# Four units' attention values in one run of matmuls per tile, and loads held back by sums: a fused window attention and MoE kernel

## The chip, the cores and the metric

One core of a Trainium2 chip runs the whole program. The metric is the device time of one execution in microseconds (us), as the median of several runs. The profile is one execution of the same program. Engines: PE (matmuls), DVE (vector), ACT (activations), POOL (GpSimd), SP (issues DMAs).

## The reference

```python
q, k, v: (8, 8, 576, 64) float32        # batch, heads, sequence, head size
scores = q @ k.T / 8
scores = where(|i - j| <= 32, scores, -1e9)
x = softmax(scores) @ v                 # window attention
x = x.transpose(0, 2, 1, 3).reshape(4608, 512)
h = x @ w_in                            # (512, 2048)
g = h / (1 + exp(-1.702 * h))
out = g @ w_out                         # (2048, 512)
```

## The kernel before

**Units and tiles.** The 4608 rows are cut into 36 units of 128 rows and 9 tiles of four units. Per unit: keys and queries are loaded by POOL's DMA queue (`load_kq`, L141), transposed by SP's (`T_dma`, L235; `turn(u)` does queries u and keys u + 1), `scores` makes the 24 score matmuls, ACT takes the exponential, `band` masks it on DVE, and `values` multiplies by v. v lies in `self.ve`, loaded by `load_v` (L211); a second copy shifted by 64 rows lies in `self.vo` and is made on POOL by `odd_v` (L222, two copies a unit). Each of the 8 heads of a unit is two matmuls on half the columns of PE, 65 columns long (64 values and the sum of the weights). `norm` divides on DVE (L339, L340), and `x_T` transposes x by a DMA on SP (L352) or on PE (L356).

**The MLP.** For a tile, layer 1 (`l1_group`) runs four groups, n = 0 to 3. A group has seven products of four matmuls, in the order 1, 7, 6, 2, 5, 4, 3, in the PSUM banks A, C, B and E: ACT copies product 1 from A to B and product 7 out of C, DVE writes E = B + s7 (L484, after product 6) and C = B + s7 (L490, after product 5), and ACT makes the Gelu of A, E, C, B (L471). Product 5 writes B again, so it waits until L484 has read it; product 3 waits for L490 in the same way. Sums of x (`x_sums`, L400 and L401, once a tile) and of g (`g_sums`, L412 to L415, four after each group) feed these products and those of layer 2. Layer 2 is a list `self.l2` of single matmuls, worked off in portions: `do(l2, n)` issues the next n. It uses banks LA and LB.

**Order.** Everything is written out by hand; each engine does its instructions in this order. `front(t)` makes the scores of the next four units among 32 layer 2 matmuls; `back(t)` runs the four groups of tile t and, between them, the values of the next tile's units. With u = 4t + 4, `back` handles units u to u + 3. `SHARES` gives the layer 2 matmuls dealt out after products 1, 7, 2 and 5/4 (`fill(1)`, `fill(7)`, `fill(2)`, `fill(4)`); `side(0)` and `side(1)` put one DVE step (a mask or a sum) behind L484 and L490. `AHEAD` deals some before and after the values. Banks are shared: `values(u, "AC")` fills banks A and C, which the groups use for products, and `"t"` a double bank which the scores use as well. In tiles 3 to 7 the values of two units are one run ahead of group 1, and those of the other two one run ahead of group 3; in tile 2 each of the four is a run by itself.

**Loads.** `fetch(u)` issues loads of queries u, keys u + 1 and a v on POOL, as early as its place in the order and free buffers allow (five for queries and keys each, nine for v). POOL and SP work off their queues in order, so a copy or a DMA that waits holds all that stand behind it.

Of the kernel before, what the change touches and what calls it, by code (L numbers as in the profile page):

```python
# [15 lines left out]
F32 = mybir.dt.float32  # L16
BF16 = mybir.dt.bfloat16
F16 = mybir.dt.float16
# [8 lines left out]
class _Kernel:  # L27
# [55 lines left out]
    def setup(self):  # L83
        nc, cst = self.nc, self.cst
        self.ident = cst.tile([128, 128], BF16, name="ident")
        self.identh = cst.tile([128, 128], F16, name="identh")
        self.mask = cst.tile([128, 4, SQ], BF16, name="mask")
        self.bias = cst.tile([128, 512], BF16, name="bias")
        self.w1 = cst.tile([128, 4, self.DFF], F16, name="w1")
        self.w2 = cst.tile([128, 16, self.DM], F16, name="w2")  # L90
        self.a = {i: cst.tile([128, 2, 1024], F16, name=f"a{i}") for i in (1, 2, 3, 4)}
        self.b = {i: cst.tile([128, 8, 256], F16, name=f"b{i}") for i in (1, 2, 3, 4)}
        self.k_first = cst.tile([128, 4, 64], BF16, name="k_first")
        self.v_first = cst.tile([64, self.H, 66], BF16, name="v_first")
        self.ve = [cst.tile([128, self.H, 66], BF16, name=f"ve{i}") for i in range(9)]
        self.vo = [cst.tile([128, self.H, 66], BF16, name=f"vo{i}") for i in range(5)]
        self.spark = cst.tile([128, 1], F32, name="spark")

    def setup_mask(self):

# [105 lines left out]
    def load_v(self, u, which=slice(None)):  # L206
# [3 lines left out]
        for off, b, s, n in list(self.pieces(128 * u, 128))[which]:  # L210
            self.nc.gpsimd.dma_start(t[off:off + n, :, :self.D], self.v[b, :, s:s + n, :].rearrange("h s d -> s h d"))  # L211

    def odd_v(self, u, eng, parts=(0, 1)):

        vo = self.vo[u % (3 if u > 15 else 5)]
        nxt = self.v_first if u == self.NU - 1 else self.ve[(u + 1) % 9][0:64]

        def words(ap):
            return ap.rearrange("p h d -> p (h d)").bitcast(I32)

        for i in parts:
            eng.tensor_copy(*((words(vo[64:128]), words(self.ve[u % 9][64:128])), (words(vo[0:64]), words(nxt)))[i])  # L222
# [88 lines left out]
    def values(self, u, tag):  # L311

        D = self.D
        p = self.p.pop(u)
        if tag == "t":
            acc = self.bank(tag, name="pv")
            self.acc[u] = [acc]
            acc = [acc[:, 0], acc[:, 1]]
        else:
            acc = [self.bank(x, name="pv") for x in tag]  # L320
            self.acc[u] = [x.rearrange("p (b n) -> p b n", b=1) for x in acc]
        for h in range(self.H):
            o = slice((h % 4) * (D + 1), (h % 4 + 1) * (D + 1))
            for blk in range(2):
                vt = (self.ve[u % 9], self.vo[u % (3 if u > 15 else 5)])[blk]
                w = p[:, h % 2, h // 2 * 2 + blk, :] if len(p.shape) == 4 else p[:, h % 2, h // 4, h // 2 % 2, blk, :]
                self.mm(acc[h // 4][64 * blk:64 * blk + 64, o], w, vt[:, h, :D + 1],
                        start=(h % 4 == 0))

    def norm(self, u):  # L330
        dve, D = self.nc.vector, self.D
        x = self.x[u] = self.sb("x", [128, self.H, D], F16, 4)
        rec = self.sb("rec", [128, 2, 4, 1], F32, 3)
        at = 0
        for acc in self.acc.pop(u):
            n = acc.shape[1]
            acc = acc[:, :, 0:4 * (D + 1)].rearrange("p b (h e) -> p b h e", e=D + 1)
            r = rec[:, at:at + n]
            dve.reciprocal(r, acc[:, :, :, D:])  # L339
            dve.tensor_mul(x[:, 4 * at:4 * (at + n), :].rearrange("p (b h) d -> p b h d", b=n), acc[:, :, :, :D],  # L340
                           r.to_broadcast([128, n, 4, D]))
            at += n

    def x_T(self, u, tag=None, eng=None):
        nc = self.nc
# [198 lines left out]
    def layer2(self, pairs, last):  # L544
# [54 lines left out]
        for P in (6, 2, 4, 5, 3):  # L599
# [3 lines left out]

    SHARES = {("first", 1): (3, 0, 5, 4), ("first", 2): (0, 6, 6, 6), ("first", 3): (3, 1, 7, 7), ("last", 0): (0, 12, 6, 6),
              0: (4, 4, 6, 6), 1: (3, 3, 6, 6), 2: (0, 6, 5, 6), 3: (2, 2, 5, 5)}


    AHEAD = {1: (0, 6), 3: (2, 3)}  # L610

    def opening(self):

# [119 lines left out]
        self.x_T2(6, "t", dve)  # L733
        self.do(self.l2, 6)

    def fetch(self, u):
        self.load_kq("q", u)
        self.load_kq("k", u + 1)
        if u < 16:
            self.load_v(u + 1)  # L740
        elif u >= 18:
            self.load_v(u - 1)

    def spread(self, u):
        if 16 <= u < self.NU:
# [6 lines left out]
    @staticmethod  # L752
    def do(fs, n=99):
        for _ in range(min(n, len(fs))):
            fs.pop(0)()

    def front(self, t, late):

        l2, do = self.l2, self.do
        if t + 1 == self.NT:  # L760
            self.l2eng = self.nc.scalar
            do(late, 3)
            do(l2, 8)
            self.x_T(self.NU - 2, "t", self.l2eng)
            xs = self.x_sums(t)
            do(xs, 1)
            do(l2, 12)
            do(late)
            do(xs)
            return  # L770
        self.l2eng = self.nc.vector
        u = 4 * t + 4
        self.scores(u, "t")
        self.scores(u + 1, "AC")
        do(late, 2)
        do(l2, 20)
        do(late)
        xs = self.x_sums(t)
        do(xs, 1)
        self.scores(u + 2, "BE")  # L780
        self.scores(u + 3, "t")
        do(l2, 12)
        do(xs)

    def back(self, t):

        more = t + 1 < self.NT
        do, l2 = self.do, self.l2
        u = 4 * t + 4
        bands = [lambda i=i: self.band(u + i) for i in range(4)] if more else []  # L790
        dv = bands[0:2]
        for n in range(4):
            if (t, n) == (3, 1):
                self.turn(20)
            if (t, n) != (3, 0):
                self.turn(u + n + 4)
            if (t, n) not in ((2, 3), (3, 0), (3, 3)):
                self.fetch(u + n + 5)
            if t == 2 and n in (1, 3):
                self.values(u + n - 1, "t")  # L800
                self.norm(u + n - 1)
                self.x_T(u + n - 1)
            elif more and n in (1, 3):
                do(l2, self.AHEAD[n][0])
                self.values(u + n - 1, "AC")
                self.norm(u + n - 1)
                if u + n < self.NU - 1:
                    self.x_T(u + n - 1)
                self.values(u + n, "t")
                self.norm(u + n)  # L810
                self.x_T(u + n)
                do(l2, self.AHEAD[n][1])
            if (t, n) == (3, 0):
                self.fetch(20)
            self.spread(u + n + 2)
            if (t, n) == (3, 0):
                self.fetch(21)
            if (t, n) == (3, 3):
                self.fetch(24)

            key = ("first", n) if t == 2 else ("last", n) if not more else n
            share = dict(zip((1, 7, 2, 4), self.SHARES.get(key, (3, 3, 5, 5))))

            def fill(i):
                do(l2, share[i])
                self.l2eng = self.nc.scalar
                if t == 2 and n in (1, 3) and i == 7:
                    self.values(u + n, "t")
                    if n == 3:
                        self.norm(u + n)  # L830
                        self.x_T(u + n)
                if i == 4:
                    do(dv, 2 if (t, n) == (2, 2) else 99)

            def side(i):
                if (t, n, i) == (2, 1, 0):
                    self.norm(u + n)
                    self.x_T(u + n)
                else:
                    do(dv, 1)  # L840

            self.l1_group(t, n, fill, side)
            dv += bands[2:4] if n == int(t == 2) else []
            dv += self.g_sums(t, 2 * n, 2)
        return dv

    def run(self):
# [5 lines left out]
        more = self.layer2([(i, j) for i in range(1, self.NT) for j in range(2)][:-1], (self.NT - 1, 1))  # L853
        do = self.do
# [42 lines left out]
        self.seed2 = dve  # L897
        self.odd_v(14, pool)
        self.odd_v(15, pool)
        self.fetch(16)  # L900
        late = self.back(2)
        for t in range(3, self.NT):
            self.front(t, late)
# [74 lines left out]
```

## Time and profile before

| | |
|---|---|
| runs | 281.67 us median of 3 (281.62 to 282.94) |
| profiled execution | 281.27 us, span of the profile 279.5 us |
| granted PE clock | 0.999 |
| busy | PE 96%, DVE 75%, ACT 70%, POOL 48% |
| a steady tile (t = 3 to 7) | 27.64 us |

In the rows of the order of time: start in us, duration, engine, line, operation, output and inputs by the program's names, shapes, and the count of merged instructions; in brackets the idle time before and what ended it. Matmuls are pipelined, so each lasts longer than the distance to the next; what a stretch costs PE is read from starts. In the kernel's names h is a bank of layer 1, o one of layer 2, pv one of values, tp one of transposes.

### The profile page before, as it was taken

Reading aid. Unit: us, or ns where it says so; the run is one execution under the profiler, and the core shown is the slowest. Engines: PE = TensorE matmul, PEld = TensorE weight load, DVE = VectorE, ACT = ScalarE, POOL = GpSimd, SP = SyncE. Lnnn points to the kernel's source line nnn. Section 1 sums busy time; section 2 is a strip of 40 time slices with the busy share of each in tenths; the row PEclk is TensorE's granted clock in tenths of the full one; section 3 lists DMA queues with packets and bytes.
Section 4 is the critical chain, followed back from the end, with each engine's and each line's share of the span. In section 5 each row is a group of like instructions: output and inputs, shape, how many; then the busy total and the mean of one; then the engine's idle time right before and its main releaser. Section 6 shows DMA issues by size and latency. Waiting matters only on the chain.

```text
span 279.5 us, 8854 instructions
## 1 busy us (share of the span) xinstructions
PE 268.2 (96%) x3632; PEld 222.6 (80%) x3632; DVE 210.9 (75%) x491; ACT 195.4 (70%) x343; POOL 133.0 (48%) x199
## 2 busy tenths in 40 slices
PE   1989999999999999999999999999999999999995
PEld 1568656776888888888888888888888888888884
DVE  3454598897997798788888887888778887945731
ACT  2586893989897588758875877687759775568411
POOL 8894695999593554635684519442520100000000
PEclk9999999999999999999999999999999999999999
DMA  8999999999999999999999999999972050202023
GB/s 88 166 204 199 178 207 165 185 136 159 131 167 140 203 120 140 172 189 115 182 194 178 126 163 159 134 183 132 168 91 85 2 115 19 77 2 75 2 104 124
DMA packets 150265, 37.61 MB, mean 135 GB/s; under 512 B 138064, under 2 KB 145872, under 8 KB 150224
## 3 DMA queue, kind: packets, MB, share of 16 engines
q0 software_dynamic: 106656, 18.42, 95.5%
q1 hardware_dynamic: 43120, 18.10, 37.9%
q8 instruction: 28, 0.46, 0.7%
q10 hardware_dynamic: 448, 0.52, 0.6%
q14 instruction: 13, 0.11, 0.1%
HBM read 36.83 MB, written 9.44 MB: 166 GB/s over the span
## 4 chain that ended last, share of the span: by engine, by line
PE 90%; DMA 4%; POOL 3%; ACT 1%; issue 1%; POOLq 0%
PE o L70 41%; PE h L70 39%; PE pv L70 4%; DMA w<-in_moe_w_in_dram 4%; PE sc L70 3%; POOL ve L211 1%; POOL kq L152 1%; PE tp L201 1%; PE tp L244 1%; ACT p L279 1%; POOL w L125 1%; PE tp L368 0%; ACT kq L67 0%; PE tp L356 0%; ACT L692 0%
## 5 line engine op out<-in xcount | busy, mean ns | idle before, releaser
L471 ACT ACTIVATE g<-h 128x512 f16<-128x512 f32 x128 | 72.2, 598 | 35.0 <-PE h L70 34.8
L222 POOL COPY vo<-ve 64x264 int32<-64x264 int32 x71 | 32.7, 461 | 79.3 <-PE pv L70 52.0
L70 PEld LDWEIGHTS <-g 128*128 128x128 f16 x576 | 54.5, 98 | 10.1
L70 PE MATMUL h<-xs,a 128*128 128x256 f16 x384 | 57.6, 272 | 0.0
L70 PEld LDWEIGHTS <-a 128*128 128x128 f16 x512 | 49.5, 98 | 9.1
L70 PE MATMUL o<-w,g 128*128 128x256 f16 (+1 forms) x320 | 55.0, 294 | 0.0
L70 PEld LDWEIGHTS <-w 128*128 128x128 f16 x496 | 47.7, 98 | 7.6 <-DMA w<-in_moe_w_in_dram 0.2
L70 PE MATMUL h<-xT,w 128*128 128x256 f16 (+1 forms) x368 | 53.5, 277 | 0.1
L70 PEld LDWEIGHTS <-gs 128*128 128x128 f16 x384 | 36.7, 98 | 4.7
L70 PE MATMUL o<-b,g 128*128 128x256 f16 x256 | 38.3, 273 | 0.0
L70 PE MATMUL o<-b,gs 128*128 128x256 f16 x256 | 37.7, 273 | 0.0
L484 DVE TENSOR_TENSOR h<-h,s 128x512 f32<-128x512 f32 x32 | 22.4, 699 | 19.8 <-PE h L70 19.1
L211 POOL DMA_DIRECT2D ve<-in_v_dram x40 | 34.3, 864 | 5.6 <-DMA w<-in_moe_w_out_dram 2.1
L279 ACT ACTIVATE p<-sc 128x512 bf16<-128x512 f32 x64 | 32.8, 618 | 1.2 <-PE sc L70 1.0
L67 ACT COPY h<-h 128x512 f32<-128x512 f32 x32 | 18.8, 588 | 16.7 <-PE h L70 16.3
L340 DVE TENSOR_TENSOR x<-pv,rec 128x256 f16<-128x256 f32 (+1 forms) x52 | 27.4, 527 | 1.8
L141 POOL DMA_DIRECT2D qst<-in_q_dram x35 | 28.2, 809 | 0.3
L490 DVE TENSOR_TENSOR h<-h,s 128x512 f32<-128x512 f32 x32 | 22.4, 699 | 6.4 <-PE h L70 6.1
L141 POOL DMA_DIRECT2D kst<-in_k_dram x31 | 26.5, 855 | 0.8 <-DMA w<-in_moe_w_out_dram 0.8
L309 DVE TENSOR_TENSOR p<-p,mask 128x1024 bf16<-128x1024 bf16 x32 | 22.3, 696 | 0.2
L67 ACT COPY s<-h 128x512 f32<-128x512 f32 x32 | 19.2, 600 | 1.2
L70 PE MATMUL h<-xs,w 128*128 128x256 f16 x128 | 19.2, 273 | 0.0
(88 smaller groups left out, 343.2 us busy)
## 6 DMA issues: line engine op xcount, KB each, us to landing
out_dram<-o_sb SPq DMA_DIRECT2D x33, 256.0 KB, 4.6
ve<-in_v_dram POOLq DMA_DIRECT2D x32, 128.0 KB, 6.9
kst<-in_k_dram POOLq DMA_DIRECT2D x25, 128.0 KB, 6.5
qst<-in_q_dram POOLq DMA_DIRECT2D x21, 128.0 KB, 5.6
w<-in_moe_w_out_dram POOLq DMA_DIRECT2D x4, 512.0 KB, 11.0
w<-in_moe_w_in_dram POOLq DMA_DIRECT2D x3, 512.0 KB, 9.9
qst<-in_q_dram POOLq DMA_DIRECT2D x7, 96.0 KB, 5.7
kq<-in_q_dram POOLq DMA_DIRECT2D x2, 256.0 KB, 5.9
```

Of the source, the lines that this page charges most:

```text
L67: (eng.copy if eng is self.nc.scalar else eng.tensor_copy)(out, in_)
L70: self.nc.tensor.matmul(out, lhsT, rhs, start=start, stop=stop, skip_group_check=True)
L125: self.nc.gpsimd.dma_start(self.w1[:, :, lo:lo + n], self.w_in[:, lo:lo + n].rearrange("(k p) f -> p k f", p=128))
L141: self.nc.gpsimd.dma_start(t[off:off + n], src[b, :, s:s + n, :].rearrange("h s d -> s h d"))
L211: self.nc.gpsimd.dma_start(t[off:off + n, :, :self.D], self.v[b, :, s:s + n, :].rearrange("h s d -> s h d"))
L222: eng.tensor_copy(*((words(vo[64:128]), words(self.ve[u % 9][64:128])), (words(vo[0:64]), words(nxt)))[i])
L279: self.nc.scalar.activation(p[:, eo].rearrange("k h s -> k (h s)"), sc[eo], AF.Exp, scale=self.scale)
L309: (eng or self.nc.vector).tensor_mul(pv, pv, msk.to_broadcast([128, 8, 2, SQ]))
L340: dve.tensor_mul(x[:, 4 * at:4 * (at + n), :].rearrange("p (b h) d -> p b h d", b=n), acc[:, :, :, :D], r.to_broadcast([128, n, 4, D]))
L471: act.activation(g[:, f, 256 * half:256 * half + 256], bank.rearrange("p (i n) -> p i n", i=2), AF.Gelu_apprx_sigmoid)
L484: dve.tensor_add(e, b, s7)
L490: dve.tensor_add(c, b, s7)
```

## The change

- In tiles 2 to 7 the values of all four units are one run of 64 matmuls ahead of group 2 (`values_four`). The 32 heads are dealt over banks A (7), E (7), C (4) and the two halves of t (7 each). In bank E they lie at the end of the bank, and the first matmul of E is 122 columns long instead of 65.
- `norm_four` divides bank by bank: A, C, E right behind the run, the two halves of t in `side(0)` and `side(1)` of group 2. x lies in one fixed tile `xn` for four units, and all four are transposed by DMA. The transposition of unit 34 on PE in the last tile's `front` is gone.
- `SHARES` is dealt anew, `AHEAD` is gone; the sum in tile 2 (64) and in later tiles (80 in `back`) stays. Masks run in group 0, the sums of a group in the next.
- From tile 2, group 1 on, loads and odd copies follow `LOADS`, behind a one-element POOL copy `seen` that reads the last sum of g of the group before. Query transposes go in other portions: units 18 and 19 together, 20 and 21, then 22 and 23; later two, one and one per tile.
- From unit 16 on the odd copies use four buffers instead of three.

```diff
-        vo = self.vo[u % (3 if u > 15 else 5)]
+    def odd(self, u):
+        return self.vo[u % 5 if u < 16 else (2, 3, 4, 0)[u % 4]]
...
+    FOUR = {"A": 0, "E": 7, "C": 14, "t0": 18, "t1": 25}
+    def four(self, tag):
+        return self.FOUR[tag], 4 if tag == "C" else 7, 512 - 7 * (self.D + 1) if tag == "E" else 0
+    def values_four(self, u):
+        D = self.D
+        p = [self.p.pop(u + i) for i in range(4)]
+        b = {tag: self.bank(tag, name="pv") for tag in "AECt"}
+        self.acc[u] = b | {"t0": b["t"][:, 0], "t1": b["t"][:, 1]}
+        for tag in self.FOUR:
+            lo, n, pad = self.four(tag)
+            for i in range(n):
+                x, h = divmod(lo + i, self.H)
+                at, more = pad + i * (D + 1), pad * (i == 0)
+                for blk in range(2):
+                    vt = (self.ve[(u + x) % 9], self.odd(u + x))[blk].rearrange("p h d -> p (h d)")
+                    self.mm(self.acc[u][tag][64 * blk:64 * blk + 64, at - more:at + D + 1],
+                            p[x][:, h % 2, h // 2 * 2 + blk, :], vt[:, h * (D + 2) - more:h * (D + 2) + D + 1],
+                            start=(i == 0))
+    def norm_four(self, u, tags, units):
+        dve, D = self.nc.vector, self.D
+        x = self.xn.rearrange("p u h d -> p (u h) d")
+        for tag in tags:
+            lo, n, pad = self.four(tag)
+            acc = self.acc[u].pop(tag)[:, pad:pad + n * (D + 1)].rearrange("p (h e) -> p h e", e=D + 1)
+            r = self.sb("rec4", [128, 7, 1], F32, 3)[:, 0:n]
+            dve.reciprocal(r, acc[:, :, D:])
+            dve.tensor_mul(x[:, lo:lo + n], acc[:, :, :D], r.to_broadcast([128, n, D]))
+        for i in units:
+            self.x[u + i] = self.xn[:, i]
+            self.x_T(u + i)
...
-    SHARES = {("first", 1): (3, 0, 5, 4), ("first", 2): (0, 6, 6, 6), ("first", 3): (3, 1, 7, 7), ("last", 0): (0, 12, 6, 6),
-              0: (4, 4, 6, 6), 1: (3, 3, 6, 6), 2: (0, 6, 5, 6), 3: (2, 2, 5, 5)}
-    AHEAD = {1: (0, 6), 3: (2, 3)}
+    SHARES = {("first", 0): (2, 3, 5, 4), ("first", 1): (2, 3, 5, 4), ("last", 0): (0, 12, 6, 6),
+              0: (4, 5, 6, 7), 1: (4, 5, 6, 7), 2: (2, 4, 5, 7), 3: (3, 4, 5, 5)}
...
+    LOADS = {(2, 1): [("kq", 8)], (2, 2): [("v", 5, 6, 7)], (2, 3): [("v", 8), ("kq", 9), ("odd", 4), ("kq", 10)],
+             (3, 0): [("kq", 7), ("odd", 1, 2, 3), ("v", 5, 6)], (3, 1): [("v", 7), ("kqv", 8)]}
...
-            self.x_T(self.NU - 2, "t", self.l2eng)
...
+            for i in {2: ((4,), (5,), (6, 7), ()), 3: ((4, 5), (6, 7), (), (8,))}.get(t, ((5, 6), (7,), (), (8,)))[n]:
+                self.turn(u + i)
+            if t == 2:
+                self.ahead("kq", *((17,), (18, 19), (), ())[n])
+            if more and n == 2:
+                self.values_four(u)
+                self.norm_four(u, ("A", "C", "E"), (0, 1))
+                do(l2, 1)
...
+                if more and n == 2:
+                    self.norm_four(u, (f"t{i}",), (2 + i,))
...
+            if more and (t > 2 or n > 0):
+                if u + n + 7 <= self.NU:
+                    c = 2 * ((n - 1) % 4) + 1
+                    self.nc.gpsimd.tensor_copy(self.seen, self.gs[t - (n == 0)][0:1, 2, c, 255:256])
+                for what, *us in self.LOADS.get((t, n)) or ([("odd", 2, 3), ("kqv", 7)], [("kqv", 8)], [("odd", 4), ("kqv", 9)],
+                                                            [("odd", 5), ("kqv", 10)])[n]:
+                    for i in us:
+                        if what == "odd":
+                            self.spread(u + i)
+                        else:
+                            self.ahead(what, u + i)
```

More of the change, by code (lines that the diff above doesn't have):

```diff
@@ L96, in setup @@
         self.vo = [cst.tile([128, self.H, 66], BF16, name=f"vo{i}") for i in range(5)]
+        self.xn = cst.tile([128, 4, self.H, self.D], F16, name="xn")
         self.spark = cst.tile([128, 1], F32, name="spark")
+        self.seen = cst.tile([1, 1], F16, name="seen")
     def setup_mask(self):
@@ L211, in load_v @@
             self.nc.gpsimd.dma_start(t[off:off + n, :, :self.D], self.v[b, :, s:s + n, :].rearrange("h s d -> s h d"))
+    def odd(self, u):
+        return self.vo[u % 5 if u < 16 else (2, 3, 4, 0)[u % 4]]
     def odd_v(self, u, eng, parts=(0, 1)):
-        vo = self.vo[u % (3 if u > 15 else 5)]
+        vo = self.odd(u)
         nxt = self.v_first if u == self.NU - 1 else self.ve[(u + 1) % 9][0:64]
@@ L324, in values @@
             for blk in range(2):
-                vt = (self.ve[u % 9], self.vo[u % (3 if u > 15 else 5)])[blk]
+                vt = (self.ve[u % 9], self.odd(u))[blk]
                 w = p[:, h % 2, h // 2 * 2 + blk, :] if len(p.shape) == 4 else p[:, h % 2, h // 4, h // 2 % 2, blk, :]
@@ L331, in norm @@
         dve, D = self.nc.vector, self.D
-        x = self.x[u] = self.sb("x", [128, self.H, D], F16, 4)
+        x = self.x[u] = self.xn[:, u % 4]
         rec = self.sb("rec", [128, 2, 4, 1], F32, 3)
@@ L734, in opening, with ahead @@
         self.do(self.l2, 6)
+    LOADS = {(2, 1): [("kq", 8)], (2, 2): [("v", 5, 6, 7)], (2, 3): [("v", 8), ("kq", 9), ("odd", 4), ("kq", 10)],
+             (3, 0): [("kq", 7), ("odd", 1, 2, 3), ("v", 5, 6)], (3, 1): [("v", 7), ("kqv", 8)]}
+    def ahead(self, what, *us):
+        for u in us:
+            if "q" in what:
+                self.load_kq("q", u)
+                self.load_kq("k", u + 1)
+            if "v" in what:
+                self.load_v(u)
     def fetch(self, u):
@@ L738, in fetch @@
         self.load_kq("k", u + 1)
[L739 to L742, printed above, removed]
+        self.load_v(u + 1)
     def spread(self, u):
@@ L790, in back @@
         bands = [lambda i=i: self.band(u + i) for i in range(4)] if more else []
-        dv = bands[0:2]
+        dv = bands
         for n in range(4):
[L793 to L821, printed above, removed]
+            for i in {2: ((4,), (5,), (6, 7), ()), 3: ((4, 5), (6, 7), (), (8,))}.get(t, ((5, 6), (7,), (), (8,)))[n]:
[6 more added lines that the diff above has]
+                do(l2, 1)
+            key = n if more else ("last", n)
+            if t == 2:
+                key = ("first", n) if n < 2 else n
             share = dict(zip((1, 7, 2, 4), self.SHARES.get(key, (3, 3, 5, 5))))
@@ L826, in fill @@
                 self.l2eng = self.nc.scalar
[L827 to L833, printed above, removed]
+                if i == 4 or more and (n, i) == (1, 7):
+                    do(dv, 99 if i == 4 else 2)
             def side(i):
-                if (t, n, i) == (2, 1, 0):
-                    self.norm(u + n)
-                    self.x_T(u + n)
+                if more and n == 2:
+                    self.norm_four(u, (f"t{i}",), (2 + i,))
                 else:
@@ L842, in back @@
             self.l1_group(t, n, fill, side)
-            dv += bands[2:4] if n == int(t == 2) else []
             dv += self.g_sums(t, 2 * n, 2)
+            if more and (t > 2 or n > 0):
[9 more added lines that the diff above has]
+                            self.ahead(what, u + i)
         return dv
@@ L899, in run @@
         self.odd_v(15, pool)
-        self.fetch(16)
+        self.ahead("kq", 16)
         late = self.back(2)
```

## The prediction

> **What bounds the kernel now.** I read the page first, then busy time by stage, then the order of time on PE, DVE and SP around the places the change touches.
>
> ```profile
> span 279.5 us, 8854 instructions
> PE 268.2 (96%) x3632; PEld 222.6 (80%) x3632; DVE 210.9 (75%) x491; ACT 195.4 (70%) x343; POOL 133.0 (48%) x199
> ...
> 128.10:155.74 27.64, 27.64 (x390) 23.91 (x394) 23.31 (x55) 20.69 (x37) 16.88 (x27) 1.00 2.28 169
> ```
>
> The last line is one steady tile (t = 4) in the view of busy time by stretch: span, then PE, PEld, DVE, ACT, POOL, then the granted clock (1.00). PE is busy for all 27.64 us of it. So in the part that the change rewrites (tiles 2 to 7) PE is the bound, and only two things count: time that PE loses between two streams of matmuls, and any wait that is long enough to stop PE. Loads, copies and norms cost nothing until they do that.
>
> The large matmuls follow each other every 0.109 us (four take 0.44, below), so lost time can be read off: the next start, minus the last group's start, minus 0.109 for each matmul of that group. First the value matmuls (pv), two units in one run, then one unit alone in tile 2:
>
> ```profile
> 110.06 0.60 PE L70 MATMUL h<-xT,a 128*128 128x256 f16 x4
> 110.59 0.22 PE L70 MATMUL pv<-ve,p 128*64 128x65 bf16 x1
> ...
> 111.25 0.83 PE L70 MATMUL o<-w,g 128*128 128x256 f16 x6
> ...
> 121.89 0.38 PE L70 MATMUL o<-b,g 128*128 128x256 f16 x2
> ...
> 122.33 0.19 PE L70 MATMUL pv<-vo,p 128*64 128x65 bf16 x1
> 122.47 0.19 PE L70 MATMUL pv<-ve,p 128*64 128x65 bf16 x1
> ...
> 122.97 0.50 PE L70 MATMUL o<-b,g 128*128 128x256 f16 x3
> ```
>
> ```profile
> 83.30 0.60 PE L70 MATMUL h<-xT,a 128*128 128x256 f16 x4
> ...
> 84.21 0.61 PE L70 MATMUL h<-xT,w 128*128 128x256 f16 x4
> ```
>
> One unit (16 matmuls) takes 84.21 - 83.30 - 0.44 = 0.47 us out of the stream. Two in one run take 111.25 - 110.06 - 0.44 = 0.75. So a unit costs 0.28, and a run costs 0.19 on top for going over to the half-width shape and back. The second run of the tile takes 122.97 - 121.89 - 0.22 = 0.86: 0.11 more, all at 122.33 to 122.47, where the matmuls enter the bank that the last Gelu has not left.
>
> **The merged run.** Four units in one run: 0.19 + 4 x 0.28 = 1.31, and 0.03 for the 57 added columns at the head of bank E (an estimate: 65 columns of a pair take 0.28 / 8 = 0.035). So 1.34.
> - Tiles 3 to 7: 0.75 + 0.86 becomes 1.34, so -0.27 each. I take it that the 0.11 goes: bank C now comes after 28 matmuls of A and E, 0.5 us into the run instead of 0.14, and 0.11 was the whole lateness.
> - Tile 2: four runs of 0.47 become one, 1.88 to 1.34, so -0.54.
>
> **The last transposes on PE.** The view of PE in the last tile:
>
> ```profile
> 238.92 0.60 PE L70 MATMUL o<-w,gs 128*128 128x256 f16 x4
> 239.36 0.39 PE L356 MATMUL tp<-identh,x 128*128 128x128 f16 x4
> 239.58 0.60 PE L70 MATMUL o<-w,gs 128*128 128x256 f16 x4
> ```
>
> Four transposes take 239.58 - 239.36 = 0.22 us of PE. Unit 34 now goes by DMA with the others, so -0.22. Its ACT copy goes too, which hides beside layer 2.
>
> **What the new filler counts do.** Layer 2 is dealt out in other portions, but in sum the same (64 matmuls in tile 2, 112 in later tiles), so no work is added. They matter where PE overwrites a bank that DVE still reads:
>
> ```profile
> 119.56 0.49 PE L70 MATMUL o<-w,g 128*128 128x256 f16 x3
> 119.93 0.60 PE L70 MATMUL h<-xs,a 128*128 128x256 f16 x4
> ...
> 88.23 0.60 PE L70 MATMUL o<-b,g 128*128 128x256 f16 x4
> 88.80 0.60 PE L70 MATMUL h<-xT,a 128*128 128x256 f16 x4
> ```
>
> With five fillers ahead of product 5 PE waits 119.93 - 119.56 - 0.33 = 0.04 for the sum E (L484); with four ahead of product 3 it waits 88.80 - 88.23 - 0.44 = 0.13 for the sum C (L490).
> - Tiles 3 to 7 have five ahead of product 5 in groups 2 and 3, before and after: 0.04 twice, unchanged.
> - Tile 2 now has five ahead of product 5 in all groups and four ahead of product 3 in groups 0 and 1: 4 x 0.04 + 2 x 0.13 = 0.42. Before, by the same reading, it lost 0.04 twice, 0.13 once and some 0.05 in group 3, 0.27 in all. So +0.15. The bounds for this term are 0 (DVE starts sooner without the norms between) and 0.3.
>
> **The new chain on DVE in group 2.** The value run now fills banks A, E, C and t at once, and group 2 wants A, then C, then E back. DVE rows:
>
> ```profile
> 110.95 0.18 DVE L339 RECIPROCAL rec<-pv 128x4 f32<-128x4 f32 x1 [0.16 <-PE pv L70]
> 111.17 0.42 DVE L340 TENSOR_TENSOR x<-pv,rec 128x256 f16<-128x256 f32 x1
> 111.51 0.17 DVE L339 RECIPROCAL rec<-pv 128x4 f32<-128x4 f32 x1
> ...
> 119.17 0.70 DVE L484 TENSOR_TENSOR h<-h,s 128x512 f32<-128x512 f32 x1
> ```
>
> Take the first value matmul as 0. Four heads were through at 110.59 + 0.14, and the reciprocal started 0.22 later; 0.06 lies between the end of L484 (119.87) and the matmul that waited for it (119.93). Seven heads of A are through at 0.25; reciprocal at 0.47; multiply at 0.69, 0.62 long (448 elements; 256 take 0.42, and the 512 of L484 take 0.70), ends 1.31; product 1 may start at 1.37. PE gets there at 111.25 - 110.59 + 0.56 + 0.03 = 1.25, and 1.36 after the one filler. So 0.01, nearly nothing, but with no room. C: a multiply holds DVE about 0.08 less than it lasts (111.17 to 111.51 for 0.42), so C ends near 1.87 and product 7 wants it at 2.0: hidden. E ends near 2.65, long before the sum that writes it at 3.6. Then the norm of half of t (0.76) and a layer 2 sum (0.34) stand on DVE ahead of the sum C, which starts at 3.6 + 0.61 + 0.76 + 0.34 = 5.3 and ends at 6.0; product 3 may start at 6.07 and PE arrives at 6.0, with its seven fillers. So +0.07 for product 3 and +0.01 for product 1: 0.08 in each of six tiles. The bounds are 0 and 0.3: if the two layer 2 copies on DVE (about 0.42 each), which end only some 0.05 us ahead of A's reciprocal, run late, all of it lands on product 1.
>
> **Loads, POOL and SP.** POOL gets 17 one-element copies that wait for DVE's sums; behind each are queued the loads and the odd copies of later units. SP gets queries 18 and 19 and 20 to 23 in larger blocks, and four x transposes in a row in group 2.
>
> ```profile
> ve<-in_v_dram POOLq DMA_DIRECT2D x32, 128.0 KB, 6.9
> ...
> 96.35 2.57 SPq L352 DMA_TRANSPOSE xT<-x  x2
> ...
> DMA to landing us min/median/max: 2.4/5.3/8.0
> ...
> 104.88 0.42 DVE L400 TENSOR_TENSOR xs<-xT 128x512 f16<-128x512 f16 x1
> ...
> 133.00 0.43 DVE L400 TENSOR_TENSOR xs<-xT 128x512 f16<-128x512 f16 x1 [0.40 <-DMA xT<-x]
> ```
>
> In the steady tiles a load is issued one and a half to two groups (8 to 11 us) before the transpose that needs it, against 6.9 us to landing. The odd copies for a value run are made at least a group ahead. The last x transpose goes out 6.9 us after the run's start, some 2 us sooner in the tile than now; the row at 133.00 shows that now it is late by 0.40 on DVE, which did not reach PE. The tight place is tile 2: group 1 begins at 83.30 + 0.44 = 83.7, the layer 2 pair in it is complete 22 matmuls (2.4) later, and Gelu, copy and store take some 2 us more (an estimate), so SP is at about 88.2; four transposes of queries and keys at 1.3 each and three of x bring the start of the last to 97.4 to 97.8. Now it is 96.35 + 1.28 = 97.6. The x differences want it at 104.3 (104.88 less what tile 2 saves), and PE can bear some 0.7 more: a landing above 7.2 us costs one for one, up to 0.8 at the longest seen, 8.0. I take 0. On the landing the Trainium skill, DMA: Bandwidth & Descriptors, section on the anatomy of one DMA on the gpsimd path, fits 2.0 us plus bytes over 436 KB per us; that would be about 2.3 us for 128 KB (an estimate from that page), a third of the 6.9 here, and by it held loads could never hold SP back. I go by the rows.
>
> **The sum.** Tiles 3 to 7: 5 x (-0.27 + 0.08) = -0.95. Tile 2: -0.54 + 0.15 + 0.08 = -0.31. Last tile: -0.22. Together -1.48 us. The profiled execution took 281.27 us, 1.77 of it around the span; -1.48 makes 279.8. It lies 0.40 below the median of the three runs (281.67), and it is a median that is forecast: **280.2 us**. What a measurement of this kernel can tell from no change is about 0.5%, 1.41 us, so 280.26 is the edge of "faster": the forecast sits on it.
>
> **Rivals.**
> - *The waits go too.* DVE keeps up, A, C and E come free in time and the 0.04 waits close. Per tile -0.27 - 0.08, tile 2 -0.54 - 0.27, last -0.22: -2.6, so 279.1. For it: the portions (six and seven fillers in groups 0 and 1) leave room there. Against: five fillers in groups 2 and 3 are kept. 15%.
> - *DVE becomes the bound in group 2.* The room ahead of product 1 is 0.01. If the copies ahead of A's norm end 0.25 later, 6 x 0.25 = 1.5 comes back: 281.7, no change. For it: DVE is 75% busy, and has two norms and the layer 2 sum in one group. Against: from sum C to sum C the same rows hold DVE for 0.61 + 0.36 + 0.68 (two copies) + 0.76 + 0.56 + 0.76 (norms of A, C, E) + 0.61 + 0.76 + 0.34 = 5.4 us, and PE for 47 x 0.109 + 1.34 = 6.5. 20%.
> - *SP's row of transposes comes late (slower).* The held loads reach SP late, so the x transposes behind the query transposes land after the x differences are due, at the fronts of tiles 3 to 8. It decides where the last one lands later than some 17 us after the value run began; with issue at 6.9 and a landing of 8.0 it is at 14.9, so SP must be held 2 us beyond that. From there it is one for one at six fronts: 0.5 us each gives 280.2 + 3.0 = 283.2, 1 us each 286.2. For it: one wait on POOL holds every load behind it, and the row at 133.00 shows this transfer last already. Against: 2 us of room gained. 13%.
>
> **How the numbers follow.** Forecast, with 279.6 to 280.8 for its bounds: 52%, a little over half of it (29 points) beyond the edge. Faster: 29 + 15 + 4 (half-late DVE that still leaves 1.41) = 48%. Within 0.5%: 23 + 16 = 39%. Slower: 13%. The range leaves out the slower rival and the lowest end of the first: 279.0 to 282.4.
>
> **What would show it.** Right: one run of 64 pv matmuls per tile that takes about 1.34 us; no transposes on PE in the last tile; steady tiles of about 27.45 instead of 27.64. The chain in group 2 is wrong if product 1 or product 3 there starts more than 0.1 us after PE is free. Wrong altogether: PE idle at a front, with the x differences (L400's successor) waiting for a DMA, or pv matmuls waiting for POOL's odd copies or a load.

## The result and the profile after

Before 281.92 us (281.14 to 282.94, six runs), after 280.06 us (279.65 to 280.19, six runs); ratio 0.993, 95% interval 0.9909 to 0.9951. The forecast was 280.2.

The page of the changed kernel:

```profile
span 278.4 us, 8851 instructions
...
L869 POOL COPY seen<-gs 1x1 f16<-1x1 f16 x17 | 3.4, 198 | 45.4 <-DVE gs L456 45.4
```

The span is 1.1 shorter than before, and POOL now stands 45.4 us ahead of the 17 holding copies, waiting for DVE's sums of g. The profiled executions differ by 1.08 us (281.27 and 280.19), the medians by 1.86. The first number is accounted for below; the rest lies between runs of which there is no trace.

Busy time by stretch, cut at the value runs of tiles 3 to 5 (span, then PE, PEld, DVE, ACT, POOL, granted clock, DMA share, GB/s):

```profile
115.51:143.68 28.17, 27.59 (x386) 23.82 (x384) 22.86 (x53) 20.94 (x37) 16.86 (x28) 1.00 2.21 160
143.68:171.10 27.42, 27.42 (x386) 23.91 (x384) 22.69 (x53) 20.78 (x37) 16.41 (x28) 1.00 1.95 172
```

A tile is 27.42 instead of 27.64, but for one: 115.51 to 143.68 takes 28.17, and PE is busy in only 27.59 of it. Tile 2, cut at the same two places of the program, in the changed kernel and in the one before:

```profile
77.59:99.63 22.04, 22.04 (x273) 18.91 (x270) 18.89 (x44) 15.88 (x30) 9.86 (x14) 1.00 1.59 154
```

```profile
77.85:100.19 22.34, 22.34 (x273) 18.90 (x270) 18.03 (x41) 16.13 (x30) 12.10 (x17) 1.00 1.98 161
```

That is -0.30. The starts (77.59 and 77.85) also say that the opening ended 0.26 sooner.

PE in the order of time around a merged run, and product 3 of that group:

```profile
115.18 0.60 PE L70 MATMUL h<-xT,a 128*128 128x256 f16 x4
115.71 0.22 PE L70 MATMUL pv<-ve,p 128*64 128x65 bf16 x1
...
116.88 0.28 PE L70 MATMUL o<-b,gs 128*128 128x256 f16 x1
117.09 0.61 PE L70 MATMUL h<-xT,w 128*128 128x256 f16 x4
...
121.38 0.49 PE L70 MATMUL o<-b,g 128*128 128x256 f16 x3
121.77 0.60 PE L70 MATMUL h<-xT,a 128*128 128x256 f16 x4
```

The run of 64 costs 116.88 - 115.18 - 0.44 = 1.26. Product 1 starts at 117.09, 0.10 after PE was free (116.88 + 0.11); product 3 waits 121.77 - 121.38 - 0.33 = 0.06. DVE shows what product 1 waits for:

```profile
116.41 0.62 DVE L380 TENSOR_TENSOR xn<-pv,rec 128x448 f16<-128x448 f32 x1
```

The norm of bank A ends at 117.03, and 0.06 later PE writes A. In the view of DVE the later steps of the chain come as the prediction had them, counted from the first value matmul: C's norm ends at 1.87 (forecast 1.87), E's at 2.64 (2.65), the sum C at 6.01 (6.0).

In the last tile no transposes are left; this answers to the rows at 239.36:

```profile
238.02 1.04 PE L70 MATMUL o<-w,gs 128*128 128x256 f16 x8
238.90 1.04 PE L70 MATMUL o<-b,g 128*128 128x256 f16 x8
```

The long stretch has one gap, at the front of tile 4. PE and DVE there, and SP ahead of it:

```profile
131.68 0.60 PE L70 MATMUL o<-w,g 128*128 128x256 f16 x4
132.86 0.50 PE L70 MATMUL h<-xT,w 128*128 128x256 f16 x3 [0.58 <-issue]
132.77 0.42 DVE L441 TENSOR_TENSOR xs<-xT 128x512 f16<-128x512 f16 x1 [0.95 <-DMA xT<-xn]
```

```profile
105.59 1.45 SPq L240 DMA_TRANSPOSE kT<-kst  x1
108.57 1.98 SPq L240 DMA_TRANSPOSE qT<-qst  x1
111.53 1.19 SPq L240 DMA_TRANSPOSE kT<-kst  x1
...
116.80 1.28 SPq L240 DMA_TRANSPOSE kT<-kst  x1
118.19 2.21 SPq L546 DMA_DIRECT2D out_dram<-o_sb  x2
120.50 6.18 SPq L393 DMA_TRANSPOSE xT<-xn  x4
...
DMA to landing us min/median/max: 6.9/7.7/8.5
```

PE waits 132.86 - 131.68 - 0.44 = 0.74, and DVE's first x difference says for what: xT by DMA. (PE's own row names no releaser; DVE's does.) On SP the transposes of queries 21 and keys 22 (108.57, 111.53) start after gaps of 1.5 and 1.0 us, so their loads, held by sums, were not there; the transposes behind them follow back to back. The second of the two stores (118.83) holds SP for another 1.56, and the four x transposes go out from 120.50. The last line is their landing.

The account of the two profiled executions: opening -0.26, tile 2 -0.30, tiles 3 to 7 five times -0.22, last tile -0.22, the gap +0.75 (0.74 by the rounded rows): -1.13, against 1.08 to 1.1 measured.

### The profile page after: what moved, and what is told of

It reads as the page before. It is cut to its first block, busy times and chain, and to the rows that moved or that the text cites. A ratio compares the mean times of both kernels' runs of the same rounds, so it can differ in the third digit from the quotient of the medians.

```text
span 278.4 us, 8851 instructions
## 1 busy us (share of the span) xinstructions
PE 266.6 (96%) x3628; PEld 222.1 (80%) x3628; DVE 210.5 (76%) x483; ACT 195.5 (70%) x342; POOL 139.3 (50%) x216
## 4 chain that ended last, share of the span: by engine, by line
PE 93%; ACT 2%; DVE 2%; issue 1%; POOL 1%; POOLq 0%
PE o L70 41%; PE h L70 40%; PE sc L70 5%; PE pv L70 4%; PE tp L179 1%; ACT p L284 1%; PE tp L203 1%; PE tp L249 1%; POOL kq L154 1%; ACT p L305 1%; DVE xn L345 1%; PE tp L409 0%; PE tp L397 0%; ACT kq L67 0%; DVE mask L113 0%
## 5 line engine op out<-in xcount | busy, mean ns | idle before, releaser
L70 PEld LDWEIGHTS <-g 128*128 128x128 f16 x576 | 55.3, 98 | 9.9
L70 PE MATMUL o<-w,g 128*128 128x256 f16 (+1 forms) x320 | 55.7, 294 | 0.0
L70 PE MATMUL o<-b,gs 128*128 128x256 f16 x256 | 39.8, 273 | 0.0
L227 POOL COPY vo<-ve 64x264 int32<-64x264 int32 x71 | 35.9, 505 | 6.4 <-PE pv L70 2.3
L70 PE MATMUL o<-b,g 128*128 128x256 f16 x256 | 37.3, 273 | 0.0
L869 POOL COPY seen<-gs 1x1 f16<-1x1 f16 x17 | 3.4, 198 | 45.4 <-DVE gs L456 45.4
L314 DVE TENSOR_TENSOR p<-p,mask 128x1024 bf16<-128x1024 bf16 x32 | 21.5, 691 | 0.3 <-ACT p L284 0.3
L67 ACT COPY o_sb<-o 128x256 f32<-128x256 f32 (+1 forms) x23 | 10.7, 464 | 12.6 <-PE o L70 12.6
```

Of the source, the lines that this page charges most:

```text
L67: (eng.copy if eng is self.nc.scalar else eng.tensor_copy)(out, in_)
L70: self.nc.tensor.matmul(out, lhsT, rhs, start=start, stop=stop, skip_group_check=True)
L314: (eng or self.nc.vector).tensor_mul(pv, pv, msk.to_broadcast([128, 8, 2, SQ]))
L869: self.nc.gpsimd.tensor_copy(self.seen, self.gs[t - (n == 0)][0:1, 2, c, 255:256])
```

## The experiments

The theory to be tested: the gain is the price of the runs that are gone, the new waits in group 2 can be covered by moving one filler (a layer 2 matmul dealt in behind a product), and the gap at tile 4's front comes from the late loads of queries 21 and keys 22. The rival: the gain comes from the new order of loads and norms, and a wait that is taken away comes back elsewhere. All runs are against the kernel before on the same chip; c0 is the changed kernel again, beside e5 to e7.

| | us | ratio, 95% interval |
|---|---|---|
| e1, run cut once | 280.62 | 0.9946 (0.9926 to 0.9965) |
| e2, cut three times | 283.16 | 1.0027 (1.0004 to 1.0051) |
| e3, no hold | 286.73 | 1.0146 (1.0103 to 1.019) |
| e4, queries 21 much sooner | 280.20 | 0.9942 (0.9917 to 0.9966) |
| e5, counts dealt anew | 284.80 | 1.0086 (1.0058 to 1.0114) |
| e6, queries 21 one load sooner | 279.91 | 0.9909 (0.9878 to 0.994) |
| e7, e5 and e6 | 284.67 | 1.0083 (1.0055 to 1.0112) |
| c0, changed again | 280.44 | 0.9927 (0.9896 to 0.9959) |
| e8, two counts | 279.63 | 0.9911 (0.9876 to 0.9946) |
| e9, e8 and e6 | 278.94 | 0.9892 (0.9859 to 0.9926) |
| e10, unit 34 on PE | 280.98 | 0.9960 (0.9936 to 0.9984) |
| e11, hold in tile 2 only | 283.12 | 1.0045 (1.0019 to 1.0072) |

### The price of a run: e1 and e2

One layer 2 matmul is put into the value run, ahead of bank C; in e2 there are three, ahead of E, C and the second half of t. They are taken from those behind the run and behind product 1.

```diff
         for tag in self.FOUR:
+            if tag == "C":                  (e1; e2: if tag in ("E", "C", "t1"))
+                self.do(self.l2, 1)
             lo, n, pad = self.four(tag)
```

> The value run of each tile is cut in two by one layer 2 matmul after bank E (taken from the fillers behind product 1 of group 2, so the work is the same). Theory (each run of values has a fixed price on PE, 0.19 us as in the kernel before): 0.19 more per tile, less the 0.09 that product 1 of group 2 waits for bank A in the changed kernel and that the cut now covers, so 6 x 0.10 = 0.6 more than the changed kernel, some 280.7 us; in the trace the two inserts sum to 0.19 more than the 1.26 of the one. Rival (the gain comes from the held loads, the number of runs does not matter): 280.1, and the two inserts sum to 1.26.

> The value run is cut in four by three layer 2 matmuls, after banks A, E and the first half of t (the three that stood behind the run and behind product 1). Theory: 3 x 0.19 more per tile, less the 0.09 at product 1: 6 x 0.48 = 2.9 more than the changed kernel, some 283.0 us, slower than before. Rival (held loads): 280.1.

PE in e1, value rows left out:

```profile
115.68 0.60 PE L70 MATMUL h<-xT,a 128*128 128x256 f16 x4
116.80 0.28 PE L70 MATMUL o<-b,gs 128*128 128x256 f16 x1
117.72 0.28 PE L70 MATMUL o<-b,gs 128*128 128x256 f16 x1
```

116.80 - 115.68 - 0.44 = 0.68 and 117.72 - 116.80 - 0.11 = 0.81: 1.49 for the same 64 matmuls, 0.22 more for one cut (0.23 by the rounded rows). In e2 the four pieces take 0.44, 0.47, 0.58 and 0.45, in sum 1.94: 0.68 more for three cuts, 0.23 each. So a run has a fixed price of 0.22 to 0.23, and in the full run of 1.26 a unit costs (1.26 - 0.22) / 4 = 0.26. The time of e2 came out as the theory had it, and the rival's 280.1 is far outside: four runs a tile instead of one cost more than the whole change had gained. The time of e1 fits too, but lies within what the changed kernel itself showed later (c0, up to 282.03); there the trace decides.

### What the hold is worth: e3 and e11

e3 leaves out the seventeen holding copies; e11 keeps them in tile 2 and group 0 of tile 3.

```diff
-                if u + n + 7 <= self.NU:
-                    c = 2 * ((n - 1) % 4) + 1
-                    self.nc.gpsimd.tensor_copy(self.seen, ...)      (e3)
-                if u + n + 7 <= self.NU:
+                if t == 2 or (t, n) == (3, 0):                       (e11)
```

> The one-element POOL copies that hold the loads back are left out; order of loads and odd copies as in the changed kernel. Theory (runs): the gain stays; queries 20 to 23 come sooner, so the 0.75 us that product 1 of tile 4's first group waits goes as well: 279.3 us, and not above 280.1. Rival (held loads): the gain goes with the holds, 281.9 us as before.

Both views were wrong: without the hold the median is over 6 us above the changed kernel's, and the kernel is slower than before. The transposes of tile 3's x by SP, their landing, and the front of tile 3 on PE and DVE:

```profile
96.68 6.59 SPq L393 DMA_TRANSPOSE xT<-xn  x4
...
DMA to landing us min/median/max: 9.0/9.2/9.5
...
107.28 0.69 PE L70 MATMUL h<-xT,w 128*128 128x256 f16 x4 [2.30 <-DMA xT<-xn]
110.62 1.03 PE L70 MATMUL h<-xs,a 128*128 128x256 f16 x4 [2.22 <-DVE xs L441]
110.14 0.43 DVE L441 TENSOR_TENSOR xs<-xT 128x512 f16<-128x512 f16 x1 [5.62 <-DMA xT<-xn]
```

The same four in the changed kernel:

```profile
93.78 5.22 SPq L393 DMA_TRANSPOSE xT<-xn  x4
...
DMA to landing us min/median/max: 2.5/3.2/6.9
```

The granted clock of e3 over the whole span, in tenths for 40 slices of 7.16 us each:

```profile
PEclk9999999999999995999999999999999999999999
```

Without the hold they go out 2.9 later and take 9.0 to 9.5 to land, and PE stands 2.30 and 2.22 us (2.46 and 2.37 counted from starts). That is the end that the third rival of the prediction had named, reached by the opposite way: loads that go too soon, not too late. A second loss follows the waits in this execution: the granted clock falls to 0.50, and from 110.62 to 115.50 PE makes 23 matmuls in 4.88 us that take 2.51 at 0.109 each. So of the 7.4 us by which this tile is longer from value run to value run (34.78 against 27.42), 4.8 are waits and 2.4 the slower clock. In e11 below PE waits 1.94 us at one place, and the clock of that stretch stays at 1.00. Five of the six executions of e3 have a mean clock of 0.987 to 0.994; the one at 1.000 took 285.05, 4.6 above c0's median, so most of the loss is there without the clock as well.

> The changed kernel with the holding copies kept in tile 2 and in group 0 of tile 3, and left out from there on. Theory: the loss of the kernel without any hold (286.7) came from the loads of tile 2, which ran beside the transposes of tile 3's x; with these held it goes, and from tile 3 on the loads are held by the buffers that they write in any case: 280.2 to 281. Rival: every tile needs the hold, and each front from tile 5 on waits 0.5 us or more: 282.5 or more.

Neither again in full. Busy time by stretch in e11, and the first x difference of tile 4 on DVE (that of tile 5 is idle 2.23 before it):

```profile
115.45:144.85 29.40, 27.61 (x386) 23.80 (x384) 23.19 (x53) 20.94 (x37) 17.98 (x26) 1.00 1.92 155
144.85:173.97 29.12, 27.92 (x387) 23.68 (x384) 22.70 (x53) 20.95 (x37) 15.35 (x23) 1.00 1.76 160
173.97:201.51 27.54, 27.54 (x386) 23.90 (x384) 22.76 (x53) 20.83 (x37) 10.86 (x17) 1.00 1.63 154
```

```profile
133.93 0.42 DVE L441 TENSOR_TENSOR xs<-xT 128x512 f16<-128x512 f16 x1 [2.10 <-DMA xT<-xn]
```

Tile 3's front waits no more on PE, so most of e3's loss did come from the loads of tile 2. But these stretches, to the value runs of tiles 4 and 5, take 29.40 and 29.12, and only from the third on, where few loads are left (POOL 10.86), does it not matter. The cleanest comparison is the row of x transposes behind 143 us, which SP begins at 147.7 to 147.8 in both. The first landing is the changed kernel's, the second that of e11:

```profile
DMA to landing us min/median/max: 2.5/3.4/5.0
```

```profile
DMA to landing us min/median/max: 7.1/8.5/9.9
```

So the same transposes at the same time take 5 us longer when loads are not held. What differs beside them is on POOL. From 146.70 to 153.40 the changed kernel starts no load; for most of that time POOL stands ahead of a holding copy:

```profile
152.38 0.18 POOL L869 COPY seen<-gs 1x1 f16<-1x1 f16 x1 [5.71 <-DVE gs L456]
```

e11 issues six load DMAs in that time. How they slow the transposes is not shown: in the same stretch the DMA engines are no busier (share 1.66 and 183 GB/s in e11, 1.75 and 206 in the changed kernel). The value loads issued from 126 to 160 land in a median of 8.2 us in the changed kernel and 12.9 in e11. The Trainium skill, DMA: Bandwidth & Descriptors, section on the anatomy of one DMA on the gpsimd path, has bytes alone as what varies, about 2.3 us for these 128 KB (an estimate from that page). No held or unheld median here is near it, so in these runs something beside the bytes sets most of the time.

### The gap at tile 4's front: e4, e6 and c0

Queries 21 and keys 22 are loaded before the three values of group 2 (e4, which also puts the odd copy of unit 16 behind queries 22), or only before one value, that of unit 20 (e6).

```diff
-    (2, 2): [("v", 5, 6, 7)], (2, 3): [("v", 8), ("kq", 9), ("odd", 4), ("kq", 10)]
+    (2, 2): [("kq", 9), ("v", 5, 6, 7)], (2, 3): [("v", 8), ("kq", 10), ("odd", 4)]    (e4)
+    (2, 2): [("v", 5, 6, 7)], (2, 3): [("kq", 9), ("v", 8), ("odd", 4), ("kq", 10)]    (e6)
```

> Queries 21 are loaded one group sooner (ahead of v 17 to 19), and the odd copy of unit 16 goes behind queries 22; everything else as changed. Theory (SP: the four x transposes of tile 4 stand behind the transposes of queries 21 to 23, which wait for their loads): they go out at 118.2 instead of 120.5, product 1 of tile 4 waits no more, 0.75 less: 279.3 us. Rival (the x transposes land late because the DMA engines are busy, wherever they stand on SP): the wait stays, 280.1 us.

> Of the loads only queries 21 (and keys 22) and v 20 change places, so queries 21 come 0.9 us sooner, but not while the x transposes of tile 3 are under way. Theory (both ends count: SP's row for tile 4, and loads beside the transposes for tile 3): neither front waits, 0.5 to 0.75 less than the changed kernel, some 279.4 us. Rival (the transposes of tile 4 land late whatever SP does): 280.1.

> The changed kernel as it is, on the same chip as the three above, for comparison: 280.1 us, with the 0.75 us of waiting at the front of tile 4 if that is a property of the order, and without if it was chance of one execution.

In e4 the gap at tile 4 was gone, and one at tile 3 had come, where the changed kernel's PE does not wait:

```profile
94.77 5.99 SPq L393 DMA_TRANSPOSE xT<-xn  x4
...
104.80 0.60 PE L70 MATMUL o<-w,g 128*128 128x256 f16 x4
105.78 0.61 PE L70 MATMUL h<-xs,a 128*128 128x256 f16 x4 [0.38 <-DVE xs L441]
105.16 0.55 DVE L441 TENSOR_TENSOR xs<-xT 128x512 f16<-128x512 f16 x1 [1.10 <-DMA xT<-xn]
```

With the two loads issued one group sooner, SP begins tile 3's x transposes at 94.77 instead of 93.78, and PE waits 0.54 at this place and 0.14 behind it, against the 0.75 saved. e6 moves them ahead of one load only, in group 3, and neither front waits. SP then begins tile 4's x transposes at 118.89 instead of 120.50. The stretch is whole (first row), but the earlier begin is little of the reason. DVE needs all four transposes, and the fourth goes out at nearly the same time in the changed kernel (second row) and in e6 (third):

```profile
115.54:142.96 27.42, 27.42 (x387) 23.91 (x384) 22.70 (x53) 20.78 (x37) 16.67 (x28) 1.00 1.90 172
...
124.94 1.74 SPq L393 DMA_TRANSPOSE xT<-xn  x1
...
124.51 1.20 SPq L393 DMA_TRANSPOSE xT<-xn  x1
```

It lands 7.7 after its issue in the changed kernel and 6.4 in e6. So of the 1.7 us gained, 0.4 are SP's row and 1.3 a quicker landing. Even of the 1.6 by which SP begins sooner, only 0.4 come from queries and keys; 1.2 are the two stores, which end after 1.03 in e6 and 2.21 in the changed kernel.

c0 waits at the place again, by 0.98 us (first row), e8, which has the same order of loads, by 1.25 (second row); e10, with that order too, hardly on DVE and not at all on PE (third row):

```profile
132.92 0.66 DVE L441 TENSOR_TENSOR xs<-xT 128x512 f16<-128x512 f16 x1 [1.07 <-DMA xT<-xn]
```

```profile
132.97 0.43 DVE L441 TENSOR_TENSOR xs<-xT 128x512 f16<-128x512 f16 x1 [1.39 <-DMA xT<-xn]
```

```profile
131.93 0.43 DVE L442 TENSOR_TENSOR xs<-xT 128x512 f16<-128x512 f16 x1 [0.23 <-DMA xT<-xn]
```

So the order is on the edge, and the gap is between 0 and 1.25 us in four executions. e8's fourth transpose goes out at 124.44, sooner than e6's, and its gap is the longest: it lands in 8.4. With this order of loads the fourth landed in 7.7, 7.9 and 8.4 where PE waited (the changed kernel, c0, e8), and in 7.2, 5.9, 7.9 and 5.1 where it did not (e10, e1, e2 and e5; the tiles of e2 and e5 are longer). With queries 21 sooner it landed in 6.0, 6.4, 7.2 and 7.2 (e4, e6, e7, e9), and tile 4's front never waited. That the order of loads decides is therefore likely; SP's row, the way that the theory gave for it, explains a quarter of the 1.7 us between the changed kernel and e6, and what sets the landing stays open. e6 is 0.53 below c0 on one chip; the intervals overlap, so the traces carry this verdict, not the medians alone.

### The waits in groups 2 and 3: e5, e7, e8 and e9

One filler of group 2 goes from behind product 1 to right behind the value run, ahead of product 1; one of group 3 goes from behind product 7 to behind product 2, ahead of product 5. That is e8. e5 also takes one each out of groups 0 and 1 and puts them into group 2. e7 and e9 add e6's order of loads.

```diff
-                do(l2, 1)
+                do(l2, 2)
-              0: (4, 5, 6, 7), 1: (4, 5, 6, 7), 2: (2, 4, 5, 7), 3: (3, 4, 5, 5)
+              0: (4, 5, 6, 6), 1: (4, 5, 6, 6), 2: (1, 4, 6, 8), 3: (3, 3, 6, 5)     (e5, e7, tiles 3 to 7)
+              0: (4, 5, 6, 7), 1: (4, 5, 6, 7), 2: (1, 4, 5, 7), 3: (3, 3, 6, 5)     (e8, e9)
```

> Only the portions of layer 2 are dealt anew, same total: in tiles 3 to 7 groups 0 to 3 get (4,5,6,6), (4,5,6,6), (1,4,6,8), (3,3,6,5), and two instead of one stand between the value run and product 1; tile 2 gets that second one too. Theory (what is left of the gain is lost to DVE arriving just too late, and one matmul of cover at each place is enough): the waits of product 1 (0.095), product 5 (0.03 and 0.04) and product 3 (0.065) go in tiles 3 to 7 and the first in tile 2: 5 x 0.23 + 0.1 = 1.2 less than the changed kernel, some 278.9 us. Rival (DVE or ACT is the bound of the group, so the wait moves to product 7, product 6 or to product 3 of groups 0 and 1): 280.1.

> Both edits together: the new portions and queries 21 ahead of v 20. Theory: they add up, 1.7 to 1.95 less than the changed kernel, some 278.2 us. Rival (the fronts are now reached sooner, so that the transposes are late again): 278.9 or more.

e5 was far off. PE and DVE in group 2 of e5:

```profile
117.20 0.60 PE L70 MATMUL h<-xT,w 128*128 128x256 f16 x4
118.83 0.27 PE L70 MATMUL o<-b,gs 128*128 128x256 f16 x1 [1.03 <-DVE o L67]
118.35 0.42 DVE L67 COPY o<-o 128x256 f32<-128x256 f32 x1
118.69 0.42 DVE L67 COPY s7o<-o 128x256 f32<-128x256 f32 x1
```

The short waits had gone, but with two fewer matmuls of layer 2 in groups 0 and 1, layer 2's product that these two DVE copies read ends behind the value run. The copies then stand behind the three norms on DVE, and layer 2 waits 118.83 - 117.20 - 0.44 = 1.19 for them, in each of tiles 3 to 7: 6.0 us lost. e7 lost the same. It is the end that the prediction had named for the norm chain ("if the two layer 2 copies on DVE ... run late"), caused here by the edit, and it fell on layer 2 instead of product 1.

> The changed kernel with two counts of fillers moved inside groups 2 and 3 only: in group 2 one matmul of layer 2 more directly behind the value run and one fewer behind product 1, in group 3 one moved from behind product 7 to behind product 2. Groups 0 and 1 are as in the changed kernel, so layer 2's product 7 ends ahead of the value run as there. Theory: the waits of 0.095 us at product 1 of group 2 and of 0.04 at product 5 of group 3 go in tiles 2 to 7, and the gap of 1.2 us seen with fewer fillers in groups 0 and 1 does not come: 6 x 0.13 = 0.8 us under the changed kernel, 279.4. Rival: the wait moves to the next product, and the time stays at 280.2.

> The same two counts, and queries 21 with keys 22 loaded ahead of values 20. Theory: both gains add, 0.8 from the fillers and 0.5 from the front of tile 4: 278.9. Rival: with groups that end sooner the fronts come sooner and wait for their transposes again: 279.6 or more, with a gap of 0.3 us or more at the first product 1 of a tile.

e8 keeps groups 0 and 1, and both waits went without a new one; 279.63, though its trace has the gap of 1.25 at tile 4's front. e9 has neither:

```profile
115.45:142.74 27.29, 27.29 (x387) 23.75 (x384) 22.92 (x53) 20.71 (x37) 17.35 (x29) 1.00 1.94 162
```

27.28 to 27.29 from each value run to the next, PE busy throughout, a span of 277.2 and 278.94 us (278.68 to 279.40): the two gains add as the theory said (278.9). Its ratio is the lowest of all that ran. It did not run beside the changed kernel; what compares them is the spans, 277.2 against 278.4 and 278.9 (c0), and the two gaps that are gone. Beside it on its chip ran e10, the changed kernel with 0.22 us of transposes more: 280.98 (280.11 to 281.99).

### The four transposes: e10

> The changed kernel with the transposes of unit 34 back on PE, in the last tile's front, as before the change. Theory: four transposes of 128 columns come back, 0.22 us: 280.4 to 280.5. Rival: the DMA transpose of unit 34 delays that of unit 35 behind it by more than this, and without it the last tile starts sooner: 280.0 or less.

```profile
237.60 0.39 PE L398 MATMUL tp<-identh,xn 128*128 128x128 f16 x4
237.83 0.60 PE L70 MATMUL o<-w,gs 128*128 128x256 f16 x4
```

They take 237.83 - 237.60 = 0.23 us of PE again. The median is 280.98 (280.11 to 281.99), more than 0.22 would give; the profiled execution is the fastest of the twelve and has no gap at tile 4's front. That the others have it is likely and not shown. The trace settles the term, the times do not.

## Why the prediction was right

Step by step:

- **The merged run.** Forecast 1.34, measured 1.26, and the cause is the one forecast, a price for each run. The price was put at 0.19 and is 0.22 (e1, e2); a unit was put at 0.28 and is 0.26. With that the two runs of before are 0.22 + 2 x 0.26 = 0.74 (measured 0.75) and 0.11 more; the merge saves one price and the 0.11: 0.75 + 0.86 - 1.26 = 0.35 a tile instead of 0.27.
- **The chain on DVE in group 2.** Product 3 waits 0.06 (forecast 0.07). Product 1 waits 0.10, forecast 0.01, and here one mis-sized term made the other: bank A came free 117.09 - 115.71 = 1.38 after the first value matmul (forecast 1.37), but PE, with its run 0.08 shorter, was there at 1.28 instead of 1.36. What the run gained beyond the forecast was lost again at product 1, so a tile went to 27.42, near the 27.45 of the forecast. e8 shows the wait to be removable by one filler.
- **Tile 2.** -0.30 against -0.31 as a sum. Inside it the terms differ: in groups 0 and 1 product 3 waits 0.08 where 0.13 was put, and a wait of 0.12 in group 0, ahead of another product, was not forecast.
- **Last tile.** -0.22, as forecast; e10 puts 0.23 back in its trace.
- **Loads and SP.** This term was taken as 0 and was 0.75 to 0.98 in the two traces of the changed kernel, at one front of six. In tile 2, which the prediction took for the tight place, its sum was right: the last x transpose goes out at 97.7 (forecast 97.4 to 97.8) and lands in 6.9, under the 7.2 that was the limit. The step that failed is tile 3. There the last x transpose should have gone out 6.9 after the value run began, with 2 us to spare; it went out 9.2 after (124.94 less 115.71), behind SP's row with queries 20 to 23 in blocks, and landed 7.7 later. In e6 it still goes out 8.8 after, and only the quicker landing keeps it in time. The condition that the prediction gave was good, a landing later than some 17 us after the value run began: that run began at 115.71, and DVE had its data at 132.77, 17.1 later.
- **Opening.** -0.26 was not in the sum. One trace of the kernel before doesn't tell whether it belongs to the change.

The steps that the change rewrites are worth 5 x 0.22 + 0.30 + 0.22 = 1.62 us by the trace, forecast 1.48; with the gap and the opening the profiled executions differ by 1.1. The forecast took its -1.48 from a median, and the medians fell by 1.86. That 280.06 lies so near 280.2 is therefore in part luck: a missed loss of 0.75 and a fall of the medians that no trace accounts for stand against each other.

Of the rivals, "the waits go too" was wrong as an account of this kernel and right as a possibility: in e9, the waits at products 1 and 5 are gone and product 3's 0.06 is left, at 278.94 against the 279.1 that it gave. "DVE becomes the bound" did not come in this order; e5 reached it with two fillers moved. "SP's row comes late" happened at one front, where SP was 2.3 us later than forecast; but what closed the gap in e6 was mostly the landing. e3 and e11 show the same end, x transposes that land after they are due, with no loads or fewer held.

## What to carry to other kernels

Price a change of shape on PE by the run: cut the run once and read the difference, here 0.22 us whether it was cut once or three times. When PE gets faster at a place where another engine frees a bank just in time, expect the gain back as a wait there, and look for one instruction that can be moved into it. Loads that go early are not free: ask which transposes are in flight beside them, and hold or place the loads for those; then check the next front, since a load that is moved sooner can pass its wait to the tile before, as in e4. And look at the last transfer that the consumer needs, its issue and its landing: a row that begins 1.6 us sooner may end only 0.4 sooner.

## What was not expected of the hardware

- x transposes of one row, begun by SP at the same time (147.7 to 147.8), land in a median of 3.4 us with the loads held and 8.5 without.
- The same order of DMAs up to that place gave a gap of 0, 0.75, 0.98 and 1.25 us at one front in four executions (e10, the changed kernel, c0, e8), and the fourth transpose, issued from 124.44 to 124.94 in all four, landed in 7.2 to 8.4: a transfer that lands within a microsecond of its due time is no fixed quantity.
- After two waits of PE of 2.46 and 2.37 us the granted clock was 0.50 for some 5 us (e3), which cost half as much again as the waits.
